# A fused block-sorted attention and cosine-gated MLP: zeroing moved behind the first permutation, key transfers issued together, values loaded ahead of keys, two query chunks loaded into the keys' place

## The chip, the cores and the metric

The kernel runs on one core of one Trainium2 chip. Its time is device microseconds of one execution. TensorE is PE in the profile (its weight loads PEld), VectorE DVE, ScalarE ACT, GpSimd POOL, SyncE SP. PE does matrix products and transposes, DVE and ACT read its results out of PSUM, POOL does copies and fills in SBUF and issues the software DMA queue (q0), SP and ACT issue hardware DMA queues (q1 and q10).

## The reference

```
P = sort_net                                    # [4, 8, 8, 8]
for _ in range(5):
    P = exp(P - max_row(P)); P = P / (sum_row(P) + 1e-9); P = P / (sum_col(P) + 1e-9)
k_sorted = einsum('bhij,bhjcd->bhicd', P, k_b)   # 8 blocks of 96 rows, head dim 64
v_sorted = einsum('bhij,bhjcd->bhicd', P, v_b)
scores = q_b @ k_sb.T / sqrt(64)                 # inside each block: 96 x 96
attn = softmax(scores)
x = (attn @ v_sb) -> [3072 tokens, 512]          # heads side by side
h = x @ w_in;  out = (h * cos(h)) @ w_out        # 512 -> 2048 -> 512
```

There are 4 batches, 8 heads, 768 rows, head dim 64. Inputs and output are float32 in HBM; products are in bfloat16.

## The kernel before

Tokens are worked in eight chunks n = 0 to 7 of 384 (half a batch: four blocks u = 0 to 3). A chunk goes through `qk(n, u)` (scores, row maximum and subtraction on DVE), `expo(n, u)` (exponential on ACT into one of three `p_buf`), a transpose of the weights into `pT` (by PE, `p_transpose`, or by a DMA transpose that SP issues), `av(n, u)` (weights times sorted values, normalised on DVE into `xn`), a transpose into `xT` (`x_transpose` on PE, or a DMA transpose from SP), `moe_up(n)` (eight groups of h matmuls, cosine on ACT, product `gg` on DVE) and `moe_down(n)` (eight half groups e of o matmuls, copies `o_s`, stores to `out`). While chunk n is in `moe_up` and `moe_down`, pieces of chunk n + 1's attention are put between its groups: the lists handed to `moe_up` and `moe_down` are slots, one per group, of calls to issue behind it. So the order of the work on every engine is the order of the program, written out by hand, and an engine or a queue does its instructions in that order. Waits between engines come from the tiles' reads and writes. Each DMA that POOL issues also waits for the one eight before it on that queue; the hardware DMAs of SP and ACT have eight such places too.

Batches come in two pairs, 0 and 1, then 2 and 3. Keys and values of a pair lie in `kv` (`vbuf` its first half, `kbuf` its second, 128 partitions, 64 for each batch). `v_permute` (POOL copies, line 171) writes values into `vperm` ordered by head dim. `v_next` and `w_next` / `w_two` multiply them with P into `vS`, `k_sort_0`, `k_sort_1` and `k_sort_g` (in `k_next`) multiply keys into `kTs`, which has three planes z; `keys_of` gives a score product two of them. For all but chunk 0 a score product runs over 128 rows, of which the queries' tile `q_turned` has 64 zero, so both its zero half and the keys' unused rows are filled with zeros by POOL. `k_swap` (two SP transfers, lines 378 and 379) moves 64 partitions of keys to the other 64 after the key products.

Queries of chunks 0 to 2 are loaded by one DMA (`load_q`, line 120) and turned on PE. From chunk 3 on they are loaded by eight DMAs of 48 KB (line 128) into `q_mem`, whose gaps were zeroed once by `zeros_between`, and turned by two SP DMA transposes, `q_transpose_dma` (line 141), into one of two `q_turned`. `drip` loads the second pair in twelve DMAs of 128 KB per tensor (line 94).

The first stage has five rounds of row and column normalisation on DVE, ACT and PE; round 1 of the loop over `it` holds POOL's queue for a moment (`held`, line 319), then issues three quarters of w_in, fills and permutes:

```
for z in range(3):
    load_w_in(z)
nc.gpsimd.memset(kTs[64:, 2], 0.0)
nc.gpsimd.memset(kTs[:64, 1, 0], 0.0)
nc.gpsimd.memset(vperm[:64, :D // 2 * blk], 0.0)
v_permute(slice(0, 64), D // 2, False)
```

Of the kernel before, what the change touches and what calls it, by code (L numbers as in the profile page):

```python
# [18 lines left out]
def kernel(  # L19
# [96 lines left out]
    def load_q(n):  # L116
# [6 lines left out]
        else:  # L123
            src = q[b].rearrange("h (i c) d -> c i h d", c=blk).rearrange(
                "c i (h e) d -> c i h e d", e=2)
            for i in range(IC):
                for e in range(2):
                    nc.gpsimd.dma_start(  # L128
                        out=q_heads[:, i, :, e], in_=src[:, ih * IC + i, :, e])
# [178 lines left out]
    for it in range(4):  # L308
# [8 lines left out]
        if it == 1:  # L317
# [4 lines left out]
            nc.gpsimd.memset(kTs[64:, 2], 0.0)  # L322
# [1 line left out]
            nc.gpsimd.memset(vperm[:64, :D // 2 * blk], 0.0)
# [24 lines left out]
    def k_sort_0(ih, t0, nt, eng, pool, tag):  # L349
# [11 lines left out]

    def k_sort_1(t0, eng, pool, tag):
# [13 lines left out]

    def k_swap(keys):
        nc.sync.dma_start(out=keys[:64, 2], in_=keys[64:, 0])
# [414 lines left out]
```

## Time and profile before

| | |
|---|---|
| Time before, median of 3 runs | 262.75 us (262.4 to 263.04) |
| The profiled execution's own time | 262.44 us |
| Its span | 260.6 us |
| PE busy | 235.6 us, 90% |
| DVE, ACT, POOL busy | 174.8 us (67%), 162.1 us (62%), 96.2 us (37%) |
| Mean granted PE clock | 0.939 |

The busy time of PE counts matmuls whose ends are modelled, and a matmul at half clock counts double its time. The clock has to be read beside it: PEclk is about 0.5 from slice 1 to slice 4 of 40. The chain of waits follows the work that ended last backwards, from each step to what released it. Rows of the timeline give start, length, engine, line, operation, tiles, and in brackets the engine's idle time before and what ended it.

### The profile page before, as it was taken

The page shows a single profiled execution, that of the slowest core. Times are in us where ns is not written, and L with a number is a line of the kernel's source. Part 1 is how long each engine was busy: PE and PEld are TensorE (multiplying, and loading weights), DVE is VectorE, ACT ScalarE, POOL GpSimd, SP SyncE. Part 2 cuts the span into 40 slices and gives each one's busy share as a digit, 9 for nine tenths or more (in the row PEclk, how much of TensorE's full clock was granted, in tenths as well). Part 3 has the DMA queues.
Part 4 walks back from the last instruction along what each step waited for, and adds up shares of the span by engine and source line. Part 5 has one row for each costly group of instructions (what it writes and reads, how often), then busy time and mean ns, then how long its engine had stood idle before and what let it go on. Part 6 is the DMA issues. An engine that isn't in the chain of part 4 may idle for free.

```text
span 260.6 us, 5453 instructions
## 1 busy us (share of the span) xinstructions
PE 235.6 (90%) x2195; PEld 150.5 (58%) x2195; DVE 174.8 (67%) x321; ACT 162.1 (62%) x232; POOL 96.2 (37%) x114
## 2 busy tenths in 40 slices
PE   7984799888959999999998998999989989999994
PEld 5774587655635656565565654565456546555553
DVE  5576658986563895488446895599859967843710
ACT  4465967576363893789848883767277447734610
POOL 8999900199599217995002500053000000000000
PEclk9555589999997999999999999999999999999999
DMA  5994999402999998919868839468683462051012
GB/s 56 226 195 75 182 198 230 99 0 55 207 234 119 140 161 117 176 19 84 164 145 158 53 100 134 112 102 112 144 159 66 102 129 75 4 156 55 3 40 80
DMA packets 66857, 30.41 MB, mean 117 GB/s; under 512 B 53648, under 2 KB 63376, under 8 KB 66576
## 3 DMA queue, kind: packets, MB, share of 16 engines
q0 software_dynamic: 26352, 13.64, 39.8%
q1 hardware_dynamic: 39248, 14.72, 27.2%
q10 hardware_dynamic: 1232, 1.71, 2.0%
q8 instruction: 17, 0.28, 0.4%
q14 instruction: 8, 0.07, 0.1%
HBM read 27.27 MB, written 6.29 MB: 129 GB/s over the span
## 4 chain that ended last, share of the span: by engine, by line
PE 61%; DVE 11%; ACT 9%; POOL 8%; DMA 7%; issue 3%; SPq 0%; DVEq 0%; POOLq 0%; ACTq 0%
PE h L545 26%; PE o L562 22%; DMA kTs<-kTs 5%; DVE s L454 3%; DVE mx L453 3%; ACT c L549 3%; DVE gg L552 3%; PE av L508 3%; PE sc L398 2%; PE pps L495 2%; POOL vperm L171 2%; DMA pT<-p_buf 2%; PE ks L346 2%; POOL kTs L322 2%; ACT p_buf L478 1%
## 5 line engine op out<-in xcount | busy, mean ns | idle before, releaser
L545 PE MATMUL h<-xT,w_in_t 128*128 128x384 bf16 (+1 forms) x576 | 94.0, 314 | 3.9 <-DVE gg L552 1.1
L562 PE MATMUL o<-w_out_t,gg 128*128 128x512 bf16 x368 | 87.0, 379 | 0.5 <-DVE s L454 0.5
L552 DVE TENSOR_TENSOR gg<-c,h 128x768 bf16<-128x768 f32 (+1 forms) x72 | 61.2, 860 | 33.1 <-ACT c L549 32.9
L549 ACT ACTIVATE c<-h,half_pi 128x768 f32<-128x768 f32 (+1 forms) x72 | 59.7, 830 | 32.3 <-PE h L545 29.5
L545 PEld LDWEIGHTS <-w_in_t 128*128 128x128 bf16 x576 | 53.6, 100 | 32.3 <-issue 6.0
L562 PEld LDWEIGHTS <-gg 128*128 128x128 bf16 x368 | 33.6, 98 | 33.8 <-DVE s L454 0.7
L128 POOL DMA_DIRECT2D q_mem<-in_q_dram x40 | 26.6, 674 | 56.8 <-DMA q_turned<-q_mem 56.8
L453 DVE TENSOR_REDUCE mx<-sc 96x4 f32<-96x384 f32 (+1 forms) x43 | 31.9, 742 | 9.3 <-PE sc L398 6.1
L171 POOL COPY vperm<-kv 64x1536 bf16<-64x1536 bf16 (+1 forms) x10 | 28.0, 2846 | 18.3 <-DMA kv<-in_v_dram 18.2
L454 DVE TENSOR_TENSOR s<-sc,mx 96x384 f32<-96x384 f32 (+1 forms) x43 | 32.2, 749 | 2.2
L478 ACT ACTIVATE p_buf<-s 96x768 bf16<-96x768 f32 x32 | 28.1, 898 | 6.2 <-DVE s L454 4.3
L277 ACT COPY o_s<-o 128x512 f32<-128x512 f32 (+1 forms) x20 | 11.5, 576 | 31.1 <-PE o L562 29.8
L517 DVE TENSOR_TENSOR xn<-av,r 96x512 bf16<-96x512 f32 x32 | 22.0, 686 | 1.1
L277 ACT CAST vS<-vs 96x512 bf16<-96x512 f32 (+1 forms) x28 | 17.7, 645 | 6.7 <-PE vs L421 3.7
L398 PE MATMUL sc<-kTs,q_turned 128*128 128x96 bf16 x224 | 16.1, 206 | 4.2 <-DMA kTs<-kTs 3.3
L398 PEld LDWEIGHTS <-q_turned 128*128 128x128 bf16 x224 | 12.8, 98 | 8.6 <-issue 3.9
L515 DVE RECIPROCAL r<-av 96x8 f32<-96x8 f32 x32 | 6.3, 198 | 15.7 <-PE av L508 15.5
L277 ACT CAST kTs<-ks 128x512 bf16<-128x512 f32 (+2 forms) x31 | 13.9, 456 | 2.3 <-PE ks L346 2.2
L508 PEld LDWEIGHTS <-pT 96*128 96x128 bf16 (+1 forms) x160 | 7.8, 104 | 5.3 <-DMA pT<-p_buf 2.0
L279 DVE COPY o_s<-o 128x512 f32<-128x512 f32 (+1 forms) x5 | 3.1, 629 | 11.2 <-PE o L757 8.6
L549 ACT ACT_TABLE_LOAD x8 | 10.3, 1283 | 0.6 <-ACT o_s L277 0.5
L508 PE MATMUL av<-vS,pT 96*128 96x65 bf16 (+1 forms) x160 | 8.6, 200 | 2.0 <-DMA pT<-p_buf 1.3
(91 smaller groups left out, 212.8 us busy)
## 6 DMA issues: line engine op xcount, KB each, us to landing
out_dram<-o_s SPq DMA_DIRECT2D x17, 256.0 KB, 2.5
w_in_t<-in_moe_w_in_dram POOLq DMA_DIRECT2D x4, 512.0 KB, 10.0
w_out_t<-in_moe_w_out_dram POOLq DMA_DIRECT2D x4, 512.0 KB, 11.6
q_mem<-in_q_dram POOLq DMA_DIRECT2D x40, 48.0 KB, 2.9
kv<-in_k_dram POOLq DMA_DIRECT2D x2, 768.0 KB, 13.3
kv<-in_v_dram POOLq DMA_DIRECT2D x2, 768.0 KB, 16.7
kv<-in_k_dram POOLq DMA_DIRECT2D x12, 128.0 KB, 6.7
kv<-in_v_dram POOLq DMA_DIRECT2D x12, 128.0 KB, 9.6
```

Of the source, the lines that this page charges most:

```text
L128: nc.gpsimd.dma_start(out=q_heads[:, i, :, e], in_=src[:, ih * IC + i, :, e])
L171: nc.gpsimd.tensor_copy(dst, src)
L277: eng.copy(dst, src)
L398: nc.tensor.matmul(out, q_of(n, hp)[:, x:x + 128], keys_of(n, u, h2, hp), start=True, stop=True)
L453: nc.vector.reduce_max(mx[:], scv, axis=AX.X)
L454: nc.vector.tensor_tensor(s_t[n, u][:, part[0]:part[0] + w], scv, mx.to_broadcast([blk, w, H2, blk]), op=ALU.subtract)
L478: nc.scalar.activation(dst, src, AF.Exp, scale=scale)
L508: nc.tensor.matmul(a[:w, hp, h2 * (D + 1):(h2 + 1) * (D + 1)], pt[:blk, e * blk:e * blk + w], vS[g][:, v_at(g, b2, hp, h2, ih * IC + u), : ...
L545: nc.tensor.matmul(h[:, f2, :w], w_in_t[:, kk, f * 128:(f + 1) * 128], xT[n][:, kk, lo:hi], start=(kk == 0), stop=(kk == KC - 1))
L549: nc.scalar.activation(c[:, :, :w], h[:, :, :w], AF.Sin, bias=half_pi[:, 0:1])
L552: nc.vector.tensor_tensor(gt[n, fp][:, :, lo:hi], c[:, :, :w], h[:, :, :w], op=ALU.mult)
L562: nc.tensor.matmul(o[:], gt[n, f // 2][:, f % 2, ts * 128:(ts + 1) * 128], w_out_t[:, f, :], start=(f == 0), stop=(f == FC - 1))
```

## The change

1. The zeros of the second `q_turned`, of the keys' planes and of half of `vperm` are no longer written ahead of the first `v_permute`. POOL writes them after the load of the second batch's values is issued, ahead of the second `v_permute`. Of the keys' planes only kT[0] is zeroed.
2. The planes of `kTs` are used in another order (0, 1, 2 with the middle one as the place that `k_swap` fills). Both transfers of `k_swap` now write plane 1 and read planes 0 and 2.
3. `drip(vbuf, vin_d)` moves from behind stage 1's `moe_up` to ahead of `drip(kbuf, kin_d)`, and `load_q(2)` ahead of the second `v_permute`. The third `v_permute` then stands ahead of `load_q(4)`.
4. Queries of chunks 5 and 7 are loaded into `kbuf`, zeroed for it again; `load_q(5)` stands in `moe_down(2)` and `load_q(7)` in `moe_down(3)`, each behind `hold`, a POOL copy of one column of the last `p_buf`. `load_q(6)` stands directly behind `load_q(5)`.
5. In `moe_down(3)` the last `w_next` moves one slot, and the stores go to ACT's queue. In `moe_down(4)` and `moe_down(5)` an `expo` moves one slot later.

POOL, ahead of the first permutation (`vperm<-kv`), before:

```order
L195 MEMSET vS 96x128 x2
L198 MEMSET q_turned_99 64x1568
L199 MEMSET q_turned_99 64x1568
L200 MEMSET q_turned_99 64x32
L201 MEMSET q_turned_99 64x32
L319 COPY held<-cs_159 128x1
L152 DMA w_in_t<-in_moe_w_in_dram 128x4x512 x3
L322 MEMSET kTs 64x4608
L323 MEMSET kTs 64x1536
L324 MEMSET vperm 64x3072
L171 COPY vperm<-kv 64x1536 x2
```

and now:

```order
L200 MEMSET vS 96x128 x2
L318 COPY held<-cs_155 128x1
L157 DMA w_in_t<-in_moe_w_in_dram 128x4x512 x3
L176 COPY vperm<-kv 64x1536 x2
L157 DMA w_in_t<-in_moe_w_in_dram 128x4x512
```

Seven fills have left the queue ahead of the permutation; they now stand with those of `q_turned_98` behind the load of the second batch's values. What follows on POOL there, from the last fill to the third permutation, now:

```order
L646 MEMSET vperm 64x3072
L123 DMA q_mem<-in_q_dram 96x8x256
L176 COPY vperm<-kv 64x1536 x4
L94 DMA kv<-in_v_dram 128x512 x12
L94 DMA kv<-in_k_dram 128x512 x12
L141 MEMSET q_mem 96x16x64 x2
L133 DMA q_mem<-in_q_dram 96x4x64 x8
L176 COPY vperm<-kv 128x1536 x4
```

Before, the twelve DMAs of values stood behind the eight of `q_mem`. SP at the first `k_swap`, with its waits, before and now (DMAHW5 is the landing of the first of the two):

```order
L378 DMA kTs<-kTs 64x1536 [waits DVE_49,Activation_49]
L379 DMA kTs<-kTs 64x1536 [waits DMAHW5_49]
```
```order
L374 DMA kTs<-kTs 64x1536 [waits DVE_49,Activation_49]
L375 DMA kTs<-kTs 64x1536
```

The second transfer's wait for the first is gone. ACT at the start of `moe_down(3)`, before:

```order
L478 ACTIVATE p_buf_109<-s 96x8x96
L478 ACTIVATE p_buf_111<-s 96x8x96
L277 CAST vS<-vs 96x128x4
L277 COPY o_s<-o 128x512
L478 ACTIVATE p_buf_107<-s 96x8x96
L478 ACTIVATE p_buf_109<-s 96x8x96
```

and now:

```order
L474 ACTIVATE p_buf_109<-s 96x8x96
L474 ACTIVATE p_buf_111<-s 96x8x96
L474 ACTIVATE p_buf_107<-s 96x8x96
L276 COPY o_s<-o 128x512
L574 DMA out_dram<-o_s 128x512
L276 CAST vS<-vs 96x128x4
L474 ACTIVATE p_buf_109<-s 96x8x96
```

The third exponential stands ahead of a copy and a cast, and a store's issue has come between.

```diff
+    KEPT = (5, 7)
+    def q_zeroed(n):
+        return kbuf[:blk, :2 * (QZ + D)] if n in KEPT else q_mem[:]
...
-    nc.gpsimd.memset(q_turned[1][64:, 0], 0.0)
-    nc.gpsimd.memset(q_turned[1][:64, 1], 0.0)
...
-            nc.gpsimd.memset(kTs[64:, 2], 0.0)
-            nc.gpsimd.memset(kTs[:64, 1, 0], 0.0)
-            nc.gpsimd.memset(vperm[:64, :D // 2 * blk], 0.0)
             v_permute(slice(0, 64), D // 2, False)
...
     def k_swap(keys):
-        nc.sync.dma_start(out=keys[:64, 2], in_=keys[64:, 0])
-        nc.sync.dma_start(out=keys[64:, 0], in_=keys[:64, 1])
+        nc.sync.dma_start(out=keys[:64, 1], in_=keys[64:, 0])
+        nc.sync.dma_start(out=keys[64:, 1], in_=keys[:64, 2])
...
+    def hold():
+        nc.gpsimd.tensor_copy(held[:blk], p_bufs[(cnt[0] - 1) % NP][:, 0, :1])
...
     load(vbuf, 64, vin_d[1])
-    nc.gpsimd.memset(q_turned[0][64:, 0], 0.0)
-    nc.gpsimd.memset(q_turned[0][:64, 0, QW:], 0.0)
-    nc.gpsimd.memset(q_turned[0][:64, 1], 0.0)
-    nc.gpsimd.memset(q_turned[0][64:, 1, QW:], 0.0)
-    v_permute(slice(64, 128))
+    for t in (q_turned[1], q_turned[0]):
+        nc.gpsimd.memset(t[64:, 0], 0.0)
+        nc.gpsimd.memset(t[:64, 1], 0.0)
+        nc.gpsimd.memset(t[:64, 0, QW:], 0.0)
+        nc.gpsimd.memset(t[64:, 1, QW:], 0.0)
+        if t is q_turned[1]:
+            nc.gpsimd.memset(kT[0][64:, 0], 0.0)
+            nc.gpsimd.memset(kT[0][:64, 2], 0.0)
+    nc.gpsimd.memset(vperm[:64, :D // 2 * blk], 0.0)
...
     load_q(2)
+    v_permute(slice(64, 128))
+    drip(vbuf, vin_d)
...
-    drip(vbuf, vin_d)
+    v_permute(slice(0, 128))
     load_q(4)
-    v_permute(slice(0, 128))
...
     q_transpose_dma(4)
-    load_q(5)
...
-                      (2, [(k_next, A, *B), (k_swap, kT2), (w_two,)]), (3, [(w_two,)]), (4, [(w_two,)]),
+                      (2, [(k_next, A, *B), (k_swap, kT2), (w_two,)]), (3, [(w_two,), (hold,), (zeros_between, 5), (load_q, 5)]), (4, [(w_two,)]),
...
+    load_q(6)
     q_transpose_dma(5)
-    load_q(6)
...
-    moe_down(3, [[(w_next, A, *B), (qk, 4, 3)], [(expo, 4, 2), (qk, 5, 0)],
-                 [(av, 4, 0, True), (av, 4, 1, True), (expo, 4, 3)],
+    moe_down(3, [[(qk, 4, 3), (expo, 4, 2)], [(w_next, A, *B), (qk, 5, 0), (expo, 4, 3)],
+                 [(av, 4, 0, True), (av, 4, 1, True), (hold,), (load_q, 7)],
...
-                 [(expo, 5, 1)]], mid=[(x_transpose, 4, 3, A, *B)])
+                 [(expo, 5, 1)]], nc.scalar, mid=[(x_transpose, 4, 3, A, *B)])
...
     q_transpose_dma(6)
-    load_q(7)
...
-    moe_down(4, [[(qk, 6, 0)], [(av, 5, 0), (expo, 5, 3)],
-                 [(av, 5, 1), (expo, 6, 0), (qk, 6, 1)], [(av, 5, 2)],
-                 [(av, 5, 3, True), (expo, 6, 1), (qk, 6, 2)],
+    moe_down(4, [[(qk, 6, 0)], [(av, 5, 0), (expo, 5, 3)], [(av, 5, 1), (qk, 6, 1)],
+                 [(av, 5, 2), (expo, 6, 0)], [(av, 5, 3, True), (expo, 6, 1), (qk, 6, 2)],
...
-    moe_down(5, [[(av, 6, 0)], [(av, 6, 1), (av, 6, 2), (expo, 7, 0)],
-                 [(qk, 7, 1), (av, 6, 3)], [], [(expo, 7, 1), (qk, 7, 2)],
-                 [(expo, 7, 2)]], nc.scalar)
+    moe_down(5, [[(av, 6, 0)], [(av, 6, 1), (av, 6, 2)], [(qk, 7, 1), (av, 6, 3)],
+                 [(expo, 7, 0)], [(expo, 7, 1), (qk, 7, 2)], [(expo, 7, 2)]], nc.scalar)
```

More of the change, by code (lines that the diff above doesn't have):

```diff
@@ L106 @@
     q_rows = q_mem[:, :H * QR * D].rearrange("p (h x) -> p h x", h=H)
-    q_heads = q_mem.rearrange("p (e x) -> p e x", e=2)[:, :, :QZ].rearrange(
-        "p e (i h w) -> p i h e w", i=IC, h=H2)[:, :, :, :, :D]
+    KEPT = (5, 7)
+    def q_zeroed(n):
+        return kbuf[:blk, :2 * (QZ + D)] if n in KEPT else q_mem[:]
     QW = IC * H2 * blk
@@ L125, in load_q @@
                 "c i (h e) d -> c i h e d", e=2)
+            q_heads = q_zeroed(n).rearrange("p (e x) -> p e x", e=2)[:, :, :QZ].rearrange(
+                "p e (i h w) -> p i h e w", i=IC, h=H2)[:, :, :, :, :D]
             for i in range(IC):
@@ L132, in q_of, with zeros_between @@
         return q_turned[n % 2][:, e]
-    def zeros_between():
+    def zeros_between(n):
         for x in (D, QZ):
             nc.gpsimd.memset(
-                q_mem[:, x:x + QZ].rearrange("p (x w) -> p x w", w=2 * D)[:, :, :D], 0.0)
+                q_zeroed(n)[:, x:x + QZ].rearrange("p (x w) -> p x w", w=2 * D)[:, :, :D], 0.0)
     def q_transpose_dma(n):
@@ L142, in q_transpose_dma @@
                 out=q_of(n, e)[:, :QW].rearrange("p (x c) -> p x c", c=blk),
-                in_=q_mem[:, e * QZ:(e + 1) * QZ])
+                in_=q_zeroed(n)[:, e * QZ:(e + 1) * QZ])
     w_in_t = const.tile([128, KC, Dff], BF16, name="w_in_t")
@@ L195 @@
         nc.gpsimd.memset(vS[g][:, :, D:D + 1], 1.0)
-    nc.gpsimd.memset(q_turned[1][64:, 0], 0.0)
-    nc.gpsimd.memset(q_turned[1][:64, 1], 0.0)
-    nc.gpsimd.memset(q_turned[1][:64, 0, QW:], 0.0)
-    nc.gpsimd.memset(q_turned[1][64:, 1, QW:], 0.0)
     order = const.tile([blk, blk], BF16, name="order")
@@ L358, in k_sort_0 @@
             for x in range(2):
-                copy_on(eng, kT[0][hp * D:(hp + 1) * D, x * (2 - hp), ms, ts],
+                copy_on(eng, kT[0][hp * D:(hp + 1) * D, hp + x, ms, ts],
                         psv[x * D:(x + 1) * D, hp])
@@ L366, in k_sort_1 @@
                        bds[0][:, :H].rearrange("p x i -> p (x i)"))
-        copy_on(eng, kT[1][:, :2, :, t0:t0 + 8], ps.rearrange("p t (e m) -> p e m t", e=2))
+        copy_on(eng, kT[1][:, ::2, :, t0:t0 + 8], ps.rearrange("p t (e m) -> p e m t", e=2))
     def k_sort_g(t0, eng, pool, tag):
@@ L373, in k_sort_g @@
         copy_on(
-            eng, kT2[:, :2, :, :, t0:t0 + 4].rearrange("p e b m t -> p b e m t"),
+            eng, kT2[:, ::2, :, :, t0:t0 + 4].rearrange("p e b m t -> p b e m t"),
             ps.rearrange("p t (b e m) -> p b e m t", b=2, e=2))
     def k_swap(keys):
-        nc.sync.dma_start(out=keys[:64, 2], in_=keys[64:, 0])
-        nc.sync.dma_start(out=keys[64:, 0], in_=keys[:64, 1])
+        nc.sync.dma_start(out=keys[:64, 1], in_=keys[64:, 0])
+        nc.sync.dma_start(out=keys[64:, 1], in_=keys[:64, 2])
     def keys_of(n, u, h2, hp):
         g, b2, ih = where(n)
-        z = slice(0, 3 - hp, 2 - hp)
+        z = slice(hp, hp + 2)
         if n < 2:
@@ L578, in step, with drip @@
             f(*args)
+    def drip(buf, src, lo=0, hi=12):
+        for z in range(lo, hi):
+            load_pair(buf, src, 1, z * 512, (z + 1) * 512)
     def moe_up(n, slots=(), lo=0, hi=TC):
@@ L658 @@
              mid=[(x_transpose, 1, 2, V, *B), (x_transpose, 1, 3, V, *B)])
-    def drip(buf, src, lo=0, hi=12):
-        for z in range(lo, hi):
-            load_pair(buf, src, 1, z * 512, (z + 1) * 512)
     drip(kbuf, kin_d)
-    moe_up(1, [[(v_next,), (v_next,), (zeros_between,), (load_q, 3), (q_transpose_dma, 3)],
+    moe_up(1, [[(v_next,), (v_next,), (zeros_between, 3), (load_q, 3), (q_transpose_dma, 3)],
                [(v_next,), (qk_half, 2, 0, 0)], [(v_next,)], [(v_next,), (qk_half, 2, 0, 1)],
```

## The prediction

> **What bounds the kernel now.** I read the page's head first, then the chain of waits in order of time, then the timeline where the chain leaves the tensor engine (PE), then the DMA view there. In the rows by windows the columns are the stretch, each engine's busy time, the clock granted to PE, the DMA share and GB/s.
>
> ```profile
> span 260.6 us, 5453 instructions
> PE 235.6 (90%) x2195; PEld 150.5 (58%) x2195; DVE 174.8 (67%) x321; ACT 162.1 (62%) x232; POOL 96.2 (37%) x114
> ```
> ```profile
> 31.60:34.40 2.80, 2.75 (x22) 2.59 (x22) 0.66 (x3) 1.15 (x2) 1.27 (x2) 0.50 1.20 193
> 34.40:40.00 5.60, 4.83 (x80) 4.52 (x78) 3.94 (x9) 4.16 (x9) 0.00 (x0) 0.99 1.23 203
> 75.30:78.60 3.30, 0.02 (x1) 0.01 (x1) 0.95 (x1) 1.19 (x2) 3.30 (x6) 1.00 1.43 246
> 78.60:81.70 3.10, 3.08 (x20) 1.76 (x21) 1.11 (x2) 0.16 (x1) 2.97 (x6) 0.54 1.60 106
> ```
>
> PE is busy 90% of 260.6 us, so 25 us are idle at most, and half-clock stretches come on top. A gain can only come from those. Two places stand out: the start, up to about 31.6 us, and the hole at 75.3 to 78.6, behind which the clock is 0.54 for 3.1 us.
>
> The chain of waits (start, length, what) at the start runs on GpSimd (POOL), and then the timeline of the same stretch:
>
> ```profile
> 10.90 3.93 POOL kTs L322
> ...
> 16.19 2.65 POOL vperm L324
> ...
> 21.51 2.84 POOL vperm L171
> 24.62 0.82 PE pps L495 x8
> ```
> ```profile
> 15.02 0.81 PEld L421 LDWEIGHTS <-kv 64*128 64x128 bf16 x8 [0.22 <-DMA kv<-in_v_dram]
> 18.80 5.54 POOL L171 COPY vperm<-kv 64x1536 bf16<-64x1536 bf16 x2
> 19.54 0.59 PE L393 MATMUL sc<-kTs,q_turned 64*96 64x96 bf16 x6
> 22.27 0.59 ACT L277 CAST vS<-vs 96x512 bf16<-96x512 f32 x1 [1.86 <-PE vs L421]
> 22.76 1.08 ACT L478 ACTIVATE p_buf<-s 96x768 bf16<-96x768 f32 x1
> 25.46 0.80 ACT L277 COPY pT<-pps 96x768 bf16<-96x768 bf16 x1 [0.22 <-PE pps L495]
> 26.16 1.06 ACT L478 ACTIVATE p_buf<-s 96x768 bf16<-96x768 f32 x1
> 28.19 0.80 ACT L277 COPY pT<-pps 96x768 bf16<-96x768 bf16 x1
> 51.13 11.26 POOL L171 COPY vperm<-kv 64x1536 bf16<-64x1536 bf16 x4 [18.22 <-DMA kv<-in_v_dram]
> ```
>
> The first values landed at 15.02 (that wait of PE ended with them), but POOL zeroes from 10.90 to 18.80 and permutes only then. ACT's cast at 22.27 waits 1.86 us for products of the permuted values.
>
> **Term 1, zeroing behind the first permutation.** The 7.9 us of zeroing (10.90 to 18.80) and that of q_turned leave POOL's queue ahead of the permutation, which can start when its values are in, at 15.02 instead of 18.80: 3.78 us earlier. Its pieces of 2.77 us end at 17.8 and 20.6. That is not the gain, since ACT is next. The third score's products on PE end at 20.13 (19.54 + 0.59), so the first products with permuted values end near 20.65 and ACT casts them at 20.75 to 21.34. The exponential overlaps by 0.1 and ends at 22.32. The PE transposes (0.88 with their start) end at 23.3 behind it, the pT copy (0.80) at 24.15, the next exponential (1.06) at 25.1, two casts (0.59 each, overlapping) at 26.1, and the second pT copy starts at 26.15, where it now starts at 28.19. Term 1 is **2.0 us**, bounded by 0 (a clock or a wait that does not move) and 3.8 (all of POOL's).
>
> What covers the moved zeroing: POOL idles 18.22 us before the second permutation at 51.13. Added there are 3200 elements a partition for q_turned, 3072 for kTs and 3072 for vperm; at 3.93 us for 4608 (kTs) that is 8.0 us, and the one issue of load_q(2), now ahead of that permutation, fits too. kTs is even zeroed in 3072 columns instead of 6144. Were that cover gone, the 8.0 us would push the drips, not PE. All loads behind the first permutation (w_in's fourth piece, w_out, second keys and values) are issued some 3.6 us earlier, so nothing that PE needs later falls behind its own shift of 2.0.
>
> **Term 2, both key transfers at once.** From the timeline, the chain, and the queue table of the stretch 66.0 to 73.5 (packets, MB, share of 16 engines):
>
> ```profile
> 63.14 3.74 POOL L94 DMA_DIRECT2D kv<-in_k_dram  x7
> ...
> 65.70 0.33 SPq L574 DMA_DIRECT2D out_dram<-o_s  x1
> 66.19 0.49 SPq L378 DMA_DIRECT2D kTs<-kTs  x1
> ...
> 74.92 0.40 PE L421 MATMUL vs<-bdv,vperm 128*128 128x64 bf16 x8
> 78.62 0.33 PE L398 MATMUL sc<-kTs,q_turned 128*128 128x96 bf16 x4 [3.31 <-DMA kTs<-kTs]
> ```
> ```profile
> 66.19 7.37 DMA kTs<-kTs
> 73.57 4.92 DMA kTs<-kTs
> 78.95 2.55 PE h L545 x8
> ...
> 83.86 1.30 PE h L545 x8
> ```
> ```profile
> q1 hardware_dynamic: 224, 0.46, 17.7%
> ```
>
> The second transfer waits for the first (12.3 us together), PE waits 3.31 us, and the slowed clock makes eight h matmuls take 2.55 instead of 1.30, with the smaller groups behind them about 1.5 us in all. The hole is worth 4.8 us. The changed order has no wait between the two: the source of the second (z = 2) is no longer a place that the first writes. It is issued at 66.7, still in the same hardware queue behind a 256 KB store and beside a drip that is now 24 pieces instead of 12. The q1 row says what that queue gets under the drip: store plus first transfer (0.46 MB) between about 67.7 (65.70 and an estimated 2 us of fixed latency, out of the 4.92 us that 0.19 MB took) and 73.56, that is 79 KB a us. Another 197 KB then take 2.5 us, to 76.0; at the pace inside the burst they would land by 75. PE needs them at 75.32 (74.92 + 0.40), and both move by term 1 alike. I take a remaining stall of 0.6 us and no slowed clock. Term 2 is **4.2 us**, bounds 0 and 4.8.
>
> The Trainium skill ("DMA: Bandwidth & Descriptors", Queues, rings and completion order) says that a DMA engine goes round its queues by packets, so a queue's share under load depends on turns, not on bytes. The q1 row agrees as far as it goes. By that rule the second transfer's 64 packets, a third of the 192 data packets before them, would add about 2 us, landing at 75.5: a stall of 0.2 instead of 0.6.
>
> The second pair's values now drip before the keys. At 0.53 us an issue (3.74 for seven) the 24 pieces follow the second permutation (51.13 less 3.6 to 62.4 less 3.6), so they are out by 71.5 or, where POOL waits for landings, some us later. Their users stand one and two stages on (k_next in moe_up(2), w_two in moe_down(2)); PE pays nothing. Zeroing q_mem and load_q(3) now wait behind all 24, and SP's transposes of q(3), with the stores of moe_down(1) queued behind them, wait for those loads; PE wants chunk 3 only in moe_up(2), and two store buffers cover some us. A delay beyond that would show as a wait of ACT's o_s copies.
>
> **Term 3, the later stages.** From the timeline:
>
> ```profile
> 155.15 2.58 SPq L489 DMA_TRANSPOSE pT<-p_buf  x2
> 161.24 0.43 PE L508 MATMUL av<-vS,pT 96*128 96x65 bf16 x8 [0.86 <-DMA pT<-p_buf]
> 189.70 4.06 PE L545 MATMUL h<-xT,w_in_t 128*128 128x384 bf16 x24 [1.06 <-issue]
> 192.40 1.99 DVE L552 TENSOR_TENSOR gg<-c,h 128x768 bf16<-128x768 f32 x2 [2.53 <-ACT c L549]
> 213.67 4.06 PE L545 MATMUL h<-xT,w_in_t 128*128 128x384 bf16 x24 [0.66 <-DVE s L454]
> 216.47 1.89 DVE L552 TENSOR_TENSOR gg<-c,h 128x768 bf16<-128x768 f32 x2 [2.53 <-ACT c L549]
> ```
>
> In moe_down(3) the exponential (4,2) goes ahead of a cast and a store, and the stores leave SP for ACT's queue; pT(4,3) is then issued about 0.4 us earlier with no store ahead of it: the 0.86 us go. In moe_down(4) and (5) an xT transpose is no longer behind an exponential's (about 1.25 us of SP each, half of 2.58). PE's waits of 1.06 and 0.66 go, but three h groups later (4.06 us) it meets the buffer that the vector engine (DVE) frees: gg's first half ends at 193.4 where h wanted it at 192.7, and at 217.4 against 217.1. Only 0.35 and 0.3 stay. Term 3 is **1.5 us**, bounds 0 and 2.6.
>
> **Term 4, what the query loads meet.** Chunks 5 and 7 are loaded into the keys' place, 5 and 6 back to back after the last exponential of chunk 3 (`hold`), 7 after that of chunk 4. This takes POOL's waits for transposes away, which nobody waited behind. But the loads run in new places. The timeline has the time that eight issues take; the DMA views of the whole span, of 80 to 92 and of 127 to 133 have count and median us to landing:
>
> ```profile
> 115.42 5.32 POOL L128 DMA_DIRECT2D q_mem<-in_q_dram  x8
> ```
> ```profile
> q_turned<-q_mem SPq DMA_TRANSPOSE x10, 3.7
> pT<-p_buf SPq DMA_TRANSPOSE x8, 2.7
> ```
> ```profile
> q_turned<-q_mem SPq DMA_TRANSPOSE x2, 12.5
> ```
> ```profile
> pT<-p_buf SPq DMA_TRANSPOSE x1, 4.6
> ```
>
> Transposes beside the old drip took 12.5 us to land, against a median of 3.7; a pT beside a store 4.6 against 2.7. The loads, 5.3 us each, start beside pT(3,3) and pT(4,3). I take the stretch of the nearest row, 1.9 us each: at (4,3) issue 156.0 (155.15 + 1.29 - 0.4), + 2.7 + 1.9 = 160.6 against PE's arrival at 160.4 (161.24 - 0.86), at (3,3) some 0.4 more than now. Term 4 is **-0.6 us**, bounds 0 and twice 8.8. The two copies of one column by `hold`, the zeroing in kbuf and the two ACT issues lie in idle time of POOL and ACT. The second key swap (kT2) also has a query load beside it, but no longer runs one after the other; I cost it at 0.
>
> **Sum:** 2.0 + 4.2 + 1.5 - 0.6 = 7.1 us. The span goes from 260.6 to 253.5. This profiled execution took 262.44 us, 1.84 around the span, so 255.3; the median shown is 262.75, 0.31 above it, hence **255.6 us**.
>
> **The rivals.**
> - *Swap still late* (0.15). The longer drip keeps the engines full, the second transfer lands some 3 us past PE's need, and the clock falls again. For it: the first took 7.37 us under a drip half as long. Against: each piece of a drip waits in the program for the load eight before it, in either kernel, so the backlog that a transfer meets is the same. Term 2 goes: 259.8.
> - *Everything lands* (0.10). No remaining stall, no term 4, tail gain somewhat more: 0.6 + 0.6 + 0.5 better, 253.9.
> - *The clock comes up no earlier* (0.09). It rose at 34.4, 2.7 us after the dense h matmuls began. If that instant stays while h starts 2.0 us sooner, those 2.0 us do half the work: 1.0 lost, 256.6. The Trainium skill ("TensorE: Matmul & The Clock Gate", Part 1: The HAM clock gate) has such a rule: a free-running window of about 3.4 us decides, so the rise could stay or jump a whole window. This trace shows one rise and cannot tell.
> - *Query loads stretch the transposes* (0.05), the slower side. If pT(3,3) and pT(4,3) suffer half of the 8.8 us each, PE, which arrives as they land, loses 8.8: 262.75 - 7.7 + 8.8 = 263.9. It decides from about 3.9 us a place. Against: SP's descriptors go out before `hold` lets the loads start.
> - *No effect* (0.03): the start's slack is eaten by the next wait and the swap stays.
>
> The forecast has 0.58. Faster by over 0.2% (about what a measurement of this kernel tells from no change): 0.58 + 0.15 + 0.10 + 0.09 = 0.92; within it 0.03; slower 0.05. The range of 253.0 to 259.8 holds the forecast's own (254.2 to 257.0), the two mild rivals and the edge of the late swap.
>
> **What would show it.** Term 1: the first permutation starts at 15.0 and h at 29.6. Term 2: the two kTs transfers are issued 0.5 us apart, PE's wait there is under 1 us, and no stretch with clock 0.54 follows. Term 3: no wait of PE for pT at chunk 4, the waits before h of stages 5 and 6 replaced by ones of DVE after three groups. Term 4: landing times of pT under 5 us. It is wrong if the permutation starts later than 15.5, if PE's wait for kTs stays over 2 us, or if av of chunks 3 and 4 waits longer than now.

## The result, and the profile after

The changed kernel takes 254.80 us (median of 4 runs, 254.07 to 255.56) against 262.57 us for the kernel before (4 runs, 260.17 to 263.04). The ratio is 0.9722, 95% interval 0.9656 to 0.9788: faster. A second sample, on another occasion, gave 254.24 us (6 runs, 253.50 to 254.73), ratio 0.9708 (0.9669 to 0.9747). The forecast was 255.6 us in a range of 253.0 to 259.8. Ratios leave out executions over 1.5% above a kernel's fastest (the profiled ones of z_only and zk below are such, and no size rests on them alone), so a ratio can differ from that of two medians.

The head of the page after; the profiled execution took 254.07 us:

```profile
span 252.3 us, 5431 instructions
PE 233.7 (93%) x2174; PEld 151.2 (60%) x2195; DVE 174.5 (69%) x321; ACT 161.8 (64%) x232; POOL 96.0 (38%) x118
```

The span is 8.3 us shorter and PE's busy time 1.9. The latter is a gap in the record: it holds 2174 matmuls, where before it held 2195. u_q below, with the same times from stage to stage and all 2195, has 235.6 us as before. So the time that went is idle PE time, as far as the record tells. Where it went is read from landmarks in the two timelines, the start of the first `gg` of each chunk (us):

| | first permutation | first h | chunk 1 | chunk 2 | chunk 3 | chunk 4 | chunk 5 | chunk 6 | chunk 7 | span |
|---|---|---|---|---|---|---|---|---|---|---|
| before | 18.80 | 31.66 | 74.29 | 107.92 | 138.44 | 167.68 | 192.40 | 216.47 | 238.50 | 260.64 |
| after | 14.72 | 29.64 | 72.61 | 101.22 | 131.75 | 159.97 | 184.66 | 208.36 | 230.13 | 252.26 |
| earlier by | 4.08 | 2.02 | 1.68 | 6.70 | 6.69 | 7.71 | 7.74 | 8.11 | 8.37 | 8.38 |

Three steps carry it: about 1.7 us by chunk 1, 5.0 us between chunks 1 and 2, and 1.7 us behind chunk 3. Timeline of after, the start:

```profile
14.72 5.58 POOL L176 COPY vperm<-kv 64x1536 bf16<-64x1536 bf16 x2 [4.30 <-DMA kv<-in_v_dram]
22.54 0.88 PE L495 MATMUL pps<-ident,p_buf 96*96 96x96 bf16 x8 [1.15 <-ACT p_buf L474]
...
26.18 0.80 ACT L276 COPY pT<-pps 96x768 bf16<-96x768 bf16 x1
...
29.64 1.44 PE L545 MATMUL h<-xT,w_in_t 128*128 128x192 bf16 x8 [0.45 <-DVE xT L278]
```

POOL now waits for the values themselves (4.30 us, ended by their transfer). The second pT copy starts at 26.18, the forecast's 26.15, and h at 29.64, its 29.6.

The same timeline at the keys, SP's queue and then PE, and the transfers issued between 64 and 66 (count, KB, median us to landing):

```profile
64.51 0.79 SPq L374 DMA_DIRECT2D kTs<-kTs  x1
65.34 1.47 SPq L375 DMA_DIRECT2D kTs<-kTs  x1
...
73.24 0.40 PE L417 MATMUL vs<-bdv,vperm 128*128 128x64 bf16 x8
73.59 0.33 PE L394 MATMUL sc<-kTs,q_turned 128*128 128x96 bf16 x4
73.75 1.46 PE L545 MATMUL h<-xT,w_in_t 128*128 128x384 bf16 x8
```
```profile
kTs<-kTs SPq DMA_DIRECT2D x2, 192.0 KB, 8.0
```

The two transfers go out one behind the other. The row of the scores at 73.59 has no bracket: PE does not wait where it waited 3.31 us, and the eight h matmuls that were stretched behind the hole take their usual time (1.46 by modelled ends). The slack is small: 65.34 + 8.0 is 73.3, 0.3 us ahead of PE.

The queries of chunk 3 stand behind 24 drip pieces instead of 12, and yet their transposes got shorter. Before, they were issued from 81.44 for 9.98 us and landed after 12.5. After (timeline, then the transfers issued from 80 to 92):

```profile
86.03 3.16 SPq L146 DMA_TRANSPOSE q_turned<-q_mem  x2
```
```profile
q_turned<-q_mem SPq DMA_TRANSPOSE x2, 3.7
```

For the later stages, the timeline (POOL's `hold` and load, PE at av of chunks 3 and 4, PE at h of chunk 5), the transfers from 118 to 127, and the waits (total, times, longest):

```profile
119.43 0.18 POOL L489 CAST held<-p_buf 96x1 f32<-96x1 bf16 x1 [18.25 <-ACT p_buf L474]
121.34 5.31 POOL L133 DMA_DIRECT2D kv<-in_q_dram  x8
123.54 0.68 PE L508 MATMUL av<-vS,pT 96*128 96x65 bf16 x16
...
153.54 0.42 PE L508 MATMUL av<-vS,pT 96*128 96x65 bf16 x8
...
185.66 1.62 PE L545 MATMUL h<-xT,w_in_t 128*128 128x384 bf16 x9 [0.70 <-DVE gg L552]
```
```profile
kTs<-kTs SPq DMA_DIRECT2D x2, 384.0 KB, 5.7
...
pT<-p_buf SPq DMA_TRANSPOSE x2, 3.4
```
```profile
PE h L545 <- DVE gg L552: 2.2, 5, 0.7
```

Neither of these two rows of av waits for pT, although the query load of `hold` starts beside the first; before, the second waited 0.86 us. Another av of chunk 4 still waits 0.22 us for its transpose, where it waited 0.39. The waits at the head of h in stages 5 and 6 are gone, and PE waits for DVE's `gg` instead, at most 0.7 us, as the forecast had it.

### The profile page after: what moved, and what is told of

It reads as the page before. It is cut to its first block, busy times and chain, and to the rows that moved or that the text cites. A ratio compares the mean times of both kernels' runs of the same rounds, so it can differ in the third digit from the quotient of the medians.

```text
span 252.3 us, 5431 instructions
## 1 busy us (share of the span) xinstructions
PE 233.7 (93%) x2174; PEld 151.2 (60%) x2195; DVE 174.5 (69%) x321; ACT 161.8 (64%) x232; POOL 96.0 (38%) x118
## 3 DMA queue, kind: packets, MB, share of 16 engines
q1 hardware_dynamic: 38960, 14.20, 24.7%
## 4 chain that ended last, share of the span: by engine, by line
PE 66%; DVE 14%; ACT 13%; issue 3%; DMA 2%; ACTq 0%; DVEq 0%
PE h L545 25%; PE o L562 23%; ACT c L549 4%; DVE gg L552 3%; PE av L508 3%; ACT p_buf L474 3%; DVE s L450 3%; DVE mx L449 3%; ACT L549 2%; PE pps L495 2%; PE sc L394 2%; PE sk L250 2%; DVE kTs L278 2%; PE ks L342 2%; PE o L760 1%
## 5 line engine op out<-in xcount | busy, mean ns | idle before, releaser
L545 PE MATMUL h<-xT,w_in_t 128*128 128x384 bf16 (+1 forms) x576 | 92.7, 311 | 3.3 <-DVE gg L552 2.2
L562 PE MATMUL o<-w_out_t,gg 128*128 128x512 bf16 x347 | 83.9, 379 | 1.6 <-DVE s L450 0.5
L133 POOL DMA_DIRECT2D q_mem<-in_q_dram x24 | 16.0, 674 | 0.3 <-DMA kv<-in_q_dram 0.3
L489 POOL CAST held<-p_buf 96x1 f32<-96x1 bf16 x2 | 0.4, 185 | 35.3 <-ACT p_buf L474 35.3
L133 POOL DMA_DIRECT2D kv<-in_q_dram x16 | 10.6, 673 | 0.4 <-issue 0.4
```

The lines of the kernel that those rows point to most:

```text
L133: nc.gpsimd.dma_start(out=q_heads[:, i, :, e], in_=src[:, ih * IC + i, :, e])
L545: nc.tensor.matmul(h[:, f2, :w], w_in_t[:, kk, f * 128:(f + 1) * 128], xT[n][:, kk, lo:hi], start=(kk == 0), stop=(kk == KC - 1))
L562: nc.tensor.matmul(o[:], gt[n, f // 2][:, f % 2, ts * 128:(ts + 1) * 128], w_out_t[:, f, :], start=(f == 0), stop=(f == FC - 1))
```

## The experiments

Theory: the three terms of the sum (zeroing 2.0, the two transfers 4.2, the late slots 1.5, less 0.6 for the query loads). Rivals: the swap stays late, the clock takes the gain of the start, the query loads stretch transposes. Three kernels have one part of the change alone, four have all but one, two have pairs of parts, and two look at the clock.

### Only the zeroing moved (z_only)

Before, with the `memset`s of item 1 behind the load of the second values; planes, drip and slots as before.

```
-            nc.gpsimd.memset(kTs[64:, 2], 0.0)
-            nc.gpsimd.memset(kTs[:64, 1, 0], 0.0)
-            nc.gpsimd.memset(vperm[:64, :D // 2 * blk], 0.0)
             v_permute(slice(0, 64), D // 2, False)
...
     load(vbuf, 64, vin_d[1])
+    nc.gpsimd.memset(q_turned[1][64:, 0], 0.0)
...
+    nc.gpsimd.memset(kTs[64:, 2], 0.0)
+    nc.gpsimd.memset(kTs[:64, 1, 0], 0.0)
+    nc.gpsimd.memset(vperm[:64, :D // 2 * blk], 0.0)
...
     v_permute(slice(64, 128))
```

> The kernel before with only the zeroing moved behind the load of the second batch's values (the keys' planes zeroed as before, so 2.6 us more zeroing there than in the change). My theory: the first permutation starts near 14.7 us, ACT's chain is next, h starts at 29.6, and 1.7 to 2.0 us are saved: 260.7 us. Rival A: POOL alone set the start, 3.8 us: 258.8. Rival B: the wait before qk of chunk 2 (kTs) swallows or grows with the shift, under 0.7 us saved: 262.0.

Measured: 258.98 us (4 runs, 256.61 to 264.66) against 262.00; ratio 0.9851 (0.9778 to 0.9924). The times lie far apart. By the ratio that is 3.9 us, the size of rival A; but in the profiled execution, the slowest, h starts at 29.50, 2.2 us earlier and not 3.8, so the step that the theory describes is right and rival A's is not. Where the faster executions gain more than 2 us was not profiled. PE's wait for the keys shrinks to 1.1 us. What is new is a wait further on. Timeline and the transfers issued from 78 to 106:

```profile
79.44 15.93 SPq L141 DMA_TRANSPOSE q_turned<-q_mem  x2
...
103.99 0.58 ACT L273 COPY o_s<-o 128x512 f32<-128x512 f32 x1 [7.56 <-DMA out_dram<-o_s]
104.63 0.33 PE L391 MATMUL sc<-kTs,q_turned 128*128 128x96 bf16 x4 [3.28 <-ACT o_s L273]
```
```profile
kv<-in_v_dram POOLq DMA_DIRECT2D x12, 128.0 KB, 15.5
...
q_turned<-q_mem SPq DMA_TRANSPOSE x2, 19.7
```

PE waits 3.28 us at chunk 3's scores, for a copy of ACT. These scores and the output products `o` take turns in the same two PSUM buffers, and the copy into `o_s` frees one. The copy in turn waited 7.56 us for a store: there are two `o_s` buffers, and the stores stand on SP's queue behind the transposes of chunk 3's queries, whose issue took 15.93 us. These transposes landed after 19.7, beside the twelve pieces of the values' drip in its old place. That this is the next limit behind the hole, and not a mishap of this execution, is for u_drip to show, which has the same order of loads.

### Only the planes and both transfers at once (k_only)

```
-        nc.sync.dma_start(out=keys[:64, 2], in_=keys[64:, 0])
-        nc.sync.dma_start(out=keys[64:, 0], in_=keys[:64, 1])
+        nc.sync.dma_start(out=keys[:64, 1], in_=keys[64:, 0])
+        nc.sync.dma_start(out=keys[64:, 1], in_=keys[:64, 2])
```

> The kernel before with only the planes of the keys and the two transfers changed; the same amount of zeroing, ahead of the first permutation, and the drips in their old order. My theory: the second transfer is issued 0.5 us after the first and lands about when PE needs it, PE's wait of 3.31 us and the half-clock stretch behind it go, 4.8 to 5.0 us saved: 257.7 us. Rival A (the transfers share one queue, so the second lands hardly earlier, and it was the order of the drips that helped): PE still waits 2 us or more, 0 to 2 us saved, 261.5.

Measured: 262.11 us (10 runs, 257.94 to 263.65) against 262.00; ratio 0.9904 (0.9852 to 0.9956). Timeline of the profiled execution (259.34 us):

```profile
67.15 0.49 SPq L378 DMA_DIRECT2D kTs<-kTs  x1
67.69 0.65 SPq L379 DMA_DIRECT2D kTs<-kTs  x1
...
76.17 0.33 PE L398 MATMUL sc<-kTs,q_turned 128*128 128x96 bf16 x4
...
101.18 0.58 ACT L277 COPY o_s<-o 128x512 f32<-128x512 f32 x1 [3.69 <-DMA out_dram<-o_s]
```

There is no wait for the keys, and from `gg` of chunk 1 to that of chunk 2 it takes 28.82 us instead of 33.63: 4.8 gained, all of the hole. The span is only 3.1 shorter. 0.9 us had been lost ahead of the transfers: full clock (the first h matmuls under 100 ns apart) came 4.7 us after the first h instead of 2.8, so chunk 1 is at 75.20 instead of 74.29. Another 0.7 is lost between chunks 2 and 3 (31.22 us against 30.52), where av waits for its transposes, 0.90 us at the longest, and `ks` 0.62. Over all runs the gain is about 2.5 us by the ratio, and that is a weak figure: the ten times spread over 5.7 us, and their median is that of before. The transfer is hidden, as the forecast says; how much of what it hides it saves alone, these times do not settle.

### Only the late slots (tail_only)

Item 5 alone: the slots of `moe_down(3)`, `(4)`, `(5)` and the stores on ACT's queue.

```
-    moe_down(4, [[(qk, 6, 0)], [(av, 5, 0), (expo, 5, 3)],
-                 [(av, 5, 1), (expo, 6, 0), (qk, 6, 1)], [(av, 5, 2)],
+    moe_down(4, [[(qk, 6, 0)], [(av, 5, 0), (expo, 5, 3)], [(av, 5, 1), (qk, 6, 1)],
+                 [(av, 5, 2), (expo, 6, 0)],
```

> The kernel before with only the new slots and ACT's stores in the stages 3, 4 and 5. My theory: PE's waits of 0.86, 1.06 and 0.66 us before av(4,3) and before h of stages 5 and 6 go, and 0.9, 0.4 and 0.3 us of them stay as gain, 1.6 in all: 261.0 us. Rival A: all 2.6 us are gained: 260.0. Rival B: the gain of the changed kernel in stage 3 came from where the query loads stand, so less than 0.8 us here: 261.8 or more.

Measured: 260.86 us (10 runs, 258.61 to 261.86), ratio 0.9947 (0.9908 to 0.9987). By landmarks the stages shrink by 1.02 (chunk 3 to 4), 0.00, 0.37 and 0.24 us: 1.63 together, against 1.5 in the forecast and 1.68 in the change. The new wait is where it was put:

```profile
PE h L545 <- DVE gg L552: 2.2, 5, 0.7
```

### The change with the transfers one after the other (u_serial)

The old planes and the old order of `k_swap` put back into the change.

```
-        nc.sync.dma_start(out=keys[:64, 1], in_=keys[64:, 0])
-        nc.sync.dma_start(out=keys[64:, 1], in_=keys[:64, 2])
+        nc.sync.dma_start(out=keys[:64, 2], in_=keys[64:, 0])
+        nc.sync.dma_start(out=keys[64:, 0], in_=keys[:64, 1])
```

> The changed kernel with the old planes and so the old wait between the two key transfers; all else of the change kept (drips in the new order, zeroing late). My theory: the wait of PE for kTs comes back with 3 us or more, since two landings of 7 to 8 us one after the other end near 79 and PE is there at 73.6, and a half-clock stretch follows: 5 us or more lost, 260 us. Rival (drip order or zeroing did it): under 1.5 us lost, 256.

Measured: 260.06 us (5 runs, 258.55 to 260.64), ratio 0.9911 (0.9873 to 0.9949). Timeline:

```profile
64.96 0.49 SPq L374 DMA_DIRECT2D kTs<-kTs  x1
72.25 0.47 SPq L375 DMA_DIRECT2D kTs<-kTs  x1
...
77.90 0.33 PE L394 MATMUL sc<-kTs,q_turned 128*128 128x96 bf16 x4 [3.81 <-DMA kTs<-kTs]
```

The second transfer is again issued 7.3 us behind the first, the hole is back, and chunk 1 to chunk 2 takes 34.14 us instead of 28.61. By this stage the two transfers are worth 5.5 us inside the change and 4.8 alone; by the ratios some 5 us inside (0.9911 less 0.9722) and 2.5 alone, the weak figure above.

### The change with the values' drip in its old place (u_drip)

Item 3 put back: values behind the keys and behind `load_q(3)`, `load_q(2)` behind the second permutation.

```
-    load_q(2)
     v_permute(slice(64, 128))
-    drip(vbuf, vin_d)
+    load_q(2)
...
-    v_permute(slice(0, 128))
+    drip(vbuf, vin_d)
     load_q(4)
+    v_permute(slice(0, 128))
```

> The changed kernel with the second pair's values dripped behind stage 1's up groups again, load_q(2) behind the second permutation and the third permutation behind load_q(4). My theory: what the drips' order moves is not on PE's path; the key transfers meet 12 pieces either way since each piece waits for the one eight before; within 0.5 us of the changed kernel, 254.8. Rival A: the longer drip hurts the transfers in the change, so this one is faster by 0.5 us or more. Rival B: without it load_q(4) or the third permutation comes late and PE waits: 1 us or more slower, 256.

Measured: 255.34 us (6 runs, 253.50 to 257.03), ratio 0.9782 (0.9736 to 0.9829). Timeline and transfers from 78 to 106:

```profile
78.42 12.06 SPq L146 DMA_TRANSPOSE q_turned<-q_mem  x2
...
100.52 0.58 ACT L276 COPY o_s<-o 128x512 f32<-128x512 f32 x1 [6.01 <-DMA out_dram<-o_s]
101.16 0.33 PE L394 MATMUL sc<-kTs,q_turned 128*128 128x96 bf16 x4 [1.72 <-ACT o_s L276]
...
103.85 0.38 PE L342 MATMUL ks<-bd,kv 128*128 128x128 bf16 x4 [1.06 <-ACT kTs L276]
```
```profile
q_turned<-q_mem SPq DMA_TRANSPOSE x2, 16.0
```

The wait of z_only is here too, in its chain: the transposes hold SP for 12.06 us, the stores behind them go out late, ACT's copy waits 6.01 us for one, and PE waits 1.72 us for ACT's copy. The 1.06 us at `ks`, 0.41 in the change, stand behind the same late ACT. The queries themselves are not what the scores wait for: the second transpose was issued at 80.94 and landed after 19.1 by the DMA view of its issue, at 100.0, 1.1 us before the scores start and 0.6 us after PE came to them. `gg` of chunk 2 comes 2.1 us later than in the change (103.36 against 101.22), and the span is 2.1 longer. So the theory is wrong. The size is rival B's, 1 us or more, but neither load_q(4) nor the third permutation, which it named, is in this chain. The interval of the times overlaps that of the change and the fastest execution equals the change's fastest, so the size, some 2 us, rests on this one trace.

### The change with the queries of chunks 5 and 7 loaded as before (u_q)

```
-    KEPT = (5, 7)
+    KEPT = ()
...
-  (3, [(w_two,), (hold,), (zeros_between, 5), (load_q, 5)])
+  (3, [(w_two,)])
```

with `load_q(5)`, `(6)` and `(7)` back in front of the `moe_up` they stood at.

> The changed kernel with the queries of chunks 5, 6 and 7 loaded into the one old place behind the transposes of the chunk before, as in the kernel before. My theory: those loads are waited for by nobody (PE's products of chunk 5 come 15 us and more after them), so within 0.5 us of the changed kernel: 254.8. Rival: the loads at 141 to 148 and 171 to 178 (old times) did stretch the pT transposes or o stores, 0.5 us or more lost: 255.5.

Measured: 254.48 us (6 runs, 253.39 to 254.56), ratio 0.9741 (0.9705 to 0.9778), span 252.8. That is the change's own time. In u_q POOL waits 17.49 and 24.01 us for transposes of queries before a load, in the change twice for `hold` (35.3 us in all); in neither does anything stand behind those waits that PE needs soon.

### The change without `hold` (no_hold)

```
-  (3, [(w_two,), (hold,), (zeros_between, 5), (load_q, 5)])
+  (3, [(w_two,), (zeros_between, 5), (load_q, 5)])
...
-                 [(av, 4, 0, True), (av, 4, 1, True), (hold,), (load_q, 7)],
+                 [(av, 4, 0, True), (av, 4, 1, True), (load_q, 7)],
```

> The changed kernel without the two holds: POOL zeroes and loads chunk 5 as soon as its queue and the key products allow, and chunk 7 as soon as kbuf's transposes have landed, beside the pT transposes. If the loads' 128-byte packets stretch a pT transpose that PE is about to need (the slower rival of the prediction), PE's waits before av of chunks 3 and 4 grow: 0.5 to 3 us slower, 256. My theory for the size: 1.9 us of stretch against 1 to 2 us of slack, 0 to 0.6 us: 255.1.

Measured: 258.27 us (6 runs, 256.27 to 259.25), ratio 0.9886 (0.9842 to 0.9931). Timeline and transfers from 105 to 130:

```profile
115.50 5.31 POOL L133 DMA_DIRECT2D kv<-in_q_dram  x8
120.80 3.32 POOL L133 DMA_DIRECT2D q_mem<-in_q_dram  x5
...
125.77 0.43 PE L508 MATMUL av<-vS,pT 96*128 96x65 bf16 x8 [1.41 <-DMA pT<-p_buf]
127.36 0.65 PE L508 MATMUL av<-vS,pT 96*128 96x65 bf16 x8 [1.16 <-DMA pT<-p_buf]
```
```profile
kTs<-kTs SPq DMA_DIRECT2D x2, 384.0 KB, 8.4
...
pT<-p_buf SPq DMA_TRANSPOSE x4, 5.6
```

The loads start 5.8 us earlier than in the change, run beside the transposes of chunk 3's weights, and these land after 5.6 us (2.6 for the same four in the change). PE waits for them twice, and chunk 2 to chunk 3 takes 34.23 us instead of 30.53. So the slower rival's mechanism is real: it costs 3.7 us in that stage, twice the 1.9 us that the forecast took for one place and near half of the rival's 8.8. At the other place, chunk 3 to chunk 4, 0.15 us are lost (28.37 against 28.22). The theory's 0 to 0.6 us is too low, as it took one stretch of 1.9 us and no second wait. What keeps all this out of the change is `hold`, which holds the loads behind the last exponential.

### Zeroing and transfers, the values' drip in its old place (zk)

The edits of z_only and k_only together.

> Before, with the zeroing moved and the two transfers at once, and the values' drip still in its old place behind the keys. Theory (a stage that is shortened meets the transposes of chunk 3's queries, which stand beside the values' drip and land after 12 to 20 us): no wait for kTs, gg1 to gg2 about 31 instead of 28.6, PE waits of 1.5 to 3.5 us at chunk 3's scores, 257.0. Rival (the parts simply add, 0.9851 times 0.9904 of 262): no wait over 1 us at chunk 3's scores, 255.8.

Measured: 259.91 us (4 runs, 256.43 to 262.01), ratio 0.9841 (0.9762 to 0.9920). The times were 256.43, 258.82, 261.01 (profiled) and 262.01. Timeline:

```profile
78.73 13.93 SPq L141 DMA_TRANSPOSE q_turned<-q_mem  x2
...
100.56 0.59 ACT L273 COPY o_s<-o 128x512 f32<-128x512 f32 x1 [5.92 <-DMA out_dram<-o_s]
101.20 0.33 PE L391 MATMUL sc<-kTs,q_turned 128*128 128x96 bf16 x4 [1.64 <-ACT o_s L273]
```

Chunk 1 to 2 takes 31.05 us, as the theory has it, with 1.64 us at chunk 3's scores; u_drip has 31.14 and 1.72 there. What the scores wait for is again ACT's copy behind a late store, not the queries as the theory says. The two lower times lie about the theory's 257.0, and the interval just leaves out the 0.9756 of parts that add, so the rival is unlikely rather than excluded. In this execution, of 4.5 us gained by chunk 2 only 1.6 are left at chunk 3; what that second loss is worth in others was not profiled.

### Transfers and the values' place (k_drip)

k_only with item 3's `drip(vbuf, vin_d)` ahead of the keys; the zeroing as before.

```
     load_q(2)
+    drip(vbuf, vin_d)
     expo(1, 0, True)
...
-    drip(vbuf, vin_d)
-    load_q(4)
     v_permute(slice(0, 128))
+    load_q(4)
```

> Before, with the two transfers at once and the values dripped before the keys; the zeroing stays where it was. Theory (the two transfers alone lost half their gain to late queries and late pT behind them, and the values' place is what cures it): transposes of chunk 3's queries land in under 5 us, no PE wait over 1 us up to chunk 4, gg1 to gg2 28.6, 0.982 of before, about 257.2. Rival (what takes k_only's gain is not the drip): gg1 to gg2 as in k_only and a time like it, 0.990, 259.5 or more.

Measured: 258.80 us (4 runs, 258.30 to 260.08), ratio 0.9891 (0.9829 to 0.9952). Transfers from 80 to 96 and timeline:

```profile
q_turned<-q_mem SPq DMA_TRANSPOSE x2, 5.3
```
```profile
91.81 3.74 SPq L141 DMA_TRANSPOSE q_turned<-q_mem  x2
...
210.46 1.78 PE L545 MATMUL h<-xT,w_in_t 128*128 128x384 bf16 x10 [2.08 <-issue]
```

The DMA view of the transfer that SP issued at 206.89:

```profile
xT<-xn SPq DMA_TRANSPOSE x1, 3.5
```

Chunk 1 to 2 takes 28.60 us, no wait of PE from there to chunk 4's h is over 1 us but one of 1.17 for ACT's `vS`, and the transposes land after 5.3 us: about the theory, up to there. Of 5.0 us gained by chunk 2 4.6 are left at chunk 5, and then h of stage 6 waits 2.08 us where it waited 0.66, at the place that item 5 changes. It starts as the last xT transpose lands (206.89 + 3.5 is 210.4); in the kernel before, the same transpose landed after 2.3. Why it took longer stays open. But k_only had lost little where the theory put its loss: k_drip is 0.2 us better from chunk 1 to 2 and 0.3 from chunk 2 to 3, and the two spans are 257.4 and 257.5. So with the zeroing in its old place, the values' new place is worth next to nothing. The total is between the two expectations, and the interval does not separate this kernel from k_only.

### The start of the full clock (change_again, warm_fill)

The changed kernel once more, and with five dummy matmuls in PE's gaps between 24.7 and 29.6 us.

```
+    keep_warm(2)
     p_transpose(0, 1, A, *B)
     av(0, 0, True)
+    keep_warm(1)
     av(0, 1, True)
...
     x_transpose(0, 0, V, *C)
+    keep_warm(1)
     x_transpose(0, 1, V, *C)
+    keep_warm(1)
```

> The changed kernel once more, as the measure for the one with dummy matmuls on the same chip: 254.8 within 0.8, and again a start of full clock that need not be at 33.3.

> The changed kernel with five more dummy matmuls (128x256, about 0.27 us each at the low clock: 12.45 0.80 for three in the trace of before) in the tensor engine's gaps between 24.7 and 29.6 us, where nothing else of it is changed. Nothing is left out of the computation. Theory (the clock is raised by a stretch of nearly unbroken work, wherever it comes from): the first full-clock h matmuls move from 33.3 to about 29.8, the two h groups of 1.44 and 1.48 us and the transposes between them take half, gg of chunk 1 comes about 1.8 us earlier (70.8), and the time is about 253.0. Rival 1 (the instant floats with a window of its own and the run of work has no say): first full-clock h between 32 and 36 as in the other runs, 254.8 within 0.7. Rival 2 (the dummy matmuls are in the way: each takes a buffer of the products, and av of chunk 0 waits for one): h starts 0.2 to 0.5 later and the time is 255.2.

Measured: change_again 254.24 us (253.50 to 254.73, 6 runs); warm_fill 256.07 us (254.47 to 259.66, 6 runs), ratio 0.9763 (0.9714 to 0.9811). Windows of warm_fill (stretch; busy time of PE, PEld, DVE, ACT, POOL; clock, DMA share, GB/s), then its timeline:

```profile
22.20:29.70 7.50, 6.41 (x69) 4.68 (x70) 5.98 (x10) 6.89 (x9) 7.37 (x11) 0.50 1.20 175
29.70:33.00 3.30, 3.26 (x34) 3.13 (x34) 1.02 (x2) 1.02 (x3) 3.19 (x3) 0.64 1.23 201
```
```profile
29.74 1.44 PE L545 MATMUL h<-xT,w_in_t 128*128 128x192 bf16 x8 [0.24 <-DVE xT L278]
```

PE was busy for 6.41 of 7.5 us (5.33 of 7.1 in the change) and the first h group still takes 1.44 us, half clock. So the theory's step, full clock at about 29.8, did not come. Full clock came at 32.09 instead of the 33.9 of change_again and `gg` of chunk 1 0.7 us earlier, so it isn't shown either that the dummy work has no say: one profile of each cannot tell that from the spread. The median is 1.8 us above change_again's. Rival 2's 255.2 is nearest, and h starts 0.2 us later than in change_again, as it said; but that is not what costs the time, as chunk 1 is earlier. In the profile 0.86 us are lost again between chunks 5 and 6 (24.56 against 23.70), with a new wait of 0.69 us at av. The five dummy tiles turn the rotation of the three `big` buffers for all that follows; that this causes the later loss was not tried. change_again came as expected.

## Why the prediction was right

**Term 1, zeroing: right at h, 0.3 too much behind it.** Permutation 14.72 (forecast 15.0), h 29.64 (29.6). At chunk 1 1.68 of the 2.02 us are left, because full clock came 3.67 us after the first h instead of 2.8. That is the third rival at a third of its price. The runs show no rule that ties the rise to h: taken as the first h matmuls under 100 ns apart, it came 2.35 (warm_fill), 2.8 (before), 3.7 and 4.4 (the change twice), 4.6 (z_only), 4.7 (k_only) and 6.2 us (no_hold) after the first h. The Trainium skill ("TensorE: Matmul & The Clock Gate", Part 1: The HAM clock gate) says that a free-running window of about 3.4 us decides, so that equal kernels differ in how many slow matmuls they see. The spread of 3.8 us, over kernels that also differ, is a little more than one such window; it fits that rule better than a fixed delay and does not prove it. Term 1 is therefore 2.0 us at h, and its worth behind it moves with the execution by some tenths to a microsecond.

**Term 2, both transfers: the mechanism right, the size 0.8 too low.** I took a remaining stall of 0.6 us out of a landing at 76.0 (74.0 with term 1) against PE's need at 75.32. There was no stall; the term is 5.02 by landmarks, just over the 4.8 that I gave as the hole. The mis-sized step is the pace of the second transfer under the longer drip, 79 KB a us out of the q1 row, which put it 2.5 us behind the first. It landed at 73.3 (65.34 + 8.0), 0.7 us sooner than 74.0. The first landed at 72.5 (64.51 + 8.0), 0.9 us later than I had it, and the second only 0.8 us behind it. The other estimate there, 75.5 less 2.0, meets the second landing to 0.2 us, but it too had 2 us between the two, so that agreement is luck.

**What term 2 left out: item 3 is part of it.** "PE pays nothing" for the values' new place was right, and it was half the answer. Their old place costs something once PE comes earlier: u_drip loses 2.1 us to stores that stand behind held-up transposes, and z_only and zk wait at the same scores. With the old order that store sets chunk 2: `gg` of chunk 1 comes 3.0 us sooner in u_drip than in k_only (72.22 against 75.20), that of chunk 2 only 0.7 (103.36 against 104.02). So item 3 keeps the gain of term 1 from being lost there. I had this path, stores queued behind the transposes and a wait of ACT's `o_s` copies as the sign, but looked for it in the new order only, where it did not come. I had also quoted the 12.5 us of the old transposes, and used them for term 4 instead of asking what a shorter stage would meet there.

**Term 3, the late slots: right.** 1.68 us in the change, 1.63 alone, forecast 1.5, at the three places named.

**Term 4, the query loads: zero, not -0.6.** pT of chunk 3 landed after 3.4 us, av of chunk 3 did not wait, and av of chunk 4 waited less than before. The stretch that I priced exists where nothing holds the loads back (no_hold: 3.7 us at the first place, 0.15 at the second), but `hold` keeps the loads out of them: SP's transposes were out first, as I had argued against the rival and then not used in the term. By u_q item 4 as a whole is worth nothing that can be measured.

**The sum.** 1.68 + 5.02 + 1.68 + 0 = 8.4 us against 7.1 in the forecast, for this pair of profiled executions; the medians give 7.8 and 8.1. The signs that the prediction listed came, with two small departures (the transfers were issued 0.8 us apart instead of 0.5, and 0.22 us of a wait for pT is left at chunk 4), and none of its three counter-signs. The nearest rival was "everything lands" (253.9). The time lies in the middle between it and the forecast, and in two of the four terms, no stall and no term 4, it describes what happened better than the forecast does.

## What to carry to other kernels

When a hole is closed, look up what the shortened stage runs into next, with the landing times of the transfers that its next stage needs, before giving the hole's full price to the edit. Transposes by DMA that stand beside a software drip are such a limit, and so are the stores queued behind them: move the drip to where nothing needs the queues, or hold the loads back behind the last transpose with a copy that reads what the transpose reads. What an edit is worth can depend on the others (the values' place: next to nothing in k_drip, some 2 us in u_drip), so try it alone and undo it from the whole as well.

## What the runs showed of the hardware that I had not expected

The two transposes of `q_turned` (the same bytes each time) landed after 12.5 to 16.0 us beside the values' drip of 128 KB pieces (before 12.5, k_only 13.1, u_drip 16.0). They landed after 3.7 in the change and 5.3 in k_drip, where the drip's pieces had landed before and at most the last query loads of 48 KB were on their way. Their issue holds the queue of SP as well: 9.98 to 12.06 us for the two beside the drip, 3.16 and 3.74 without it, and the stores behind them wait that long.

The granted clock of the record cannot be trusted at the start. In the profile after the windows give 1.00 from 14 us on, while its eight `pps` transposes at 22.54 take 0.88 us, as in the profile before (0.88, where the record says 0.50). The timeline of warm_fill has the same eight at half and at full clock:

```profile
22.23 0.88 PE L495 MATMUL pps<-ident,p_buf 96*96 96x96 bf16 x8 [1.16 <-ACT p_buf L474]
...
32.51 0.52 PE L495 MATMUL pps<-ident,p_buf 96*96 96x96 bf16 x8
```

So the durations of equal groups say which clock ran, and the record has to be read against them.
